# Load order of the first chunks, and the second pair's attention ahead of the feed-forward product

## The chip, the core and the metric

The kernel runs on one core of a Trainium2 chip. A core has five engines with instruction streams of their own, which meet at semaphores: TensorE (PE, matrix products; its weight loads are the row PEld), VectorE (DVE), ScalarE (ACT), GpSimd (POOL) and SyncE (SP). Each runs its own instructions in order. DMA engines move data between main memory (HBM) and the on-chip SBUF; products are collected in PSUM, in eight banks. The metric is the device time of one execution in microseconds (us).

## What is computed

Retention (linear attention with decay), written in the reference as a recurrence over 768 tokens, for 4 batches, 8 heads, head dimension 64; its result goes into a gated feed-forward layer.

```python
gamma = 1.0 - 2.0 ** (-5.0 - np.arange(H))
for t in range(S):
    state = gamma * state + einsum('bhd,bhe->bhde', k[:, :, t], v[:, :, t])
    y[:, :, t] = scale * einsum('bhd,bhde->bhe', q[:, :, t], state)
x = y.transpose(0, 2, 1, 3).reshape(3072, 512)
gate = 1 / (1 + exp(-(x @ w_gate)))     # 512 x 1536
out = (gate * (x @ w_val)) @ w_out      # 1536 x 512
```

## The kernel before

**Tiling.** Tokens are cut into 24 chunks of 128, six to a batch, and attention is done by chunk: scores of q and k within the chunk under a causal mask, times v (the *intra* product), plus q times the state of the chunks before (the *inter* product). The decay is folded into v, scaled by a table by token (tabr, tabv), and into y, multiplied by a table taby when it leaves PSUM. The feed-forward layer works on six tiles of 512 tokens, four chunks each: an *up* product by each of 12 column blocks of 128 (gate and value, wg and wv, four matmuls each; a sigmoid on ScalarE; a product on VectorE into hT), then eight half *down* products (6 matmuls each) from hT and wo. Operands are bf16, sums float32.

**The order is written by hand.** Every engine gets its instructions in the order in which the Python code issues them. After a prologue for tile 0, a loop goes over the tiles' groups (ups and downs), and `plan` names after which group of a tile a step of the attention of later chunks is put in: `step_t` (transposes of k and q, and scaling of v), `block` (scores, intra, state, inter) and `casts`.

**The prologue.** The first four chunks come in two pairs, a = 0 and a = 1 (chunks 0, 1 and 2, 3), loaded whole by `load_run` (L77): each partition holds two successive tokens of all heads. The names that matter:

- `kr`, `qr`, `vr`: the loads of a pair. Both `vr` share one buffer. `load_gate_val(s)` (L87) loads the slice s, 256 of 1536 columns, of wg and wv; `load_out` (L91) loads a quarter of wo; `load_chunk` (L62, L67, L68) loads k, q, v of a later chunk. All but the first `vr` are issued by GpSimd.
- `transpose_run` (L264, copy out L269 or L271), `scale_run` (L278; v times tabr), `scores_run` (L288), `masks_run` (L295), `inter_run` (L304), `intra_run` (L313), `state_run` (L325), `sum_run` (L332, L334), `state_out` (L208; the state cast to bf16 as zbd), `y_out_run` (L342; y times taby into xT, which the up product reads).
- `make_taby` (L144) makes taby by an exponential on ScalarE, `extend_taby` (L147) from another taby on GpSimd. ScalarE then changes its function table to sigmoid (L485).
- `up_columns` (L400) takes 256 tokens of two column blocks at once, `up` (L384) one block. `keep_on(n, warm)` (L429) issues n matmuls of the identity into a scratch bank; nobody reads them.

In the prologue before, the order of loads is vr0 (SyncE), kr0, qr0, kr1, wg and wv slice 0, vr1, qr1, slices 1 and 2, then slices 3 to 5, wo, chunks 4 to 7. Pair 0 is finished, up products of its 256 tokens begin (blocks 0 and 1), and among them pair 1 is scaled by VectorE, transposed, and brought through state, scores and intra; after blocks 2 to 5 of the first 256 tokens come blocks 0 to 5 of the second 256, and the loop begins at group 6.

Of the kernel before, what the change touches and what calls it, by code (L numbers as in the profile page):

```python
# [9 lines left out]
F32 = mybir.dt.float32  # L10
BF16 = mybir.dt.bfloat16
I32 = mybir.dt.int32
AX = mybir.ActivationFunctionType
# [4 lines left out]
def kernel(  # L18
# [10 lines left out]
    nc = tc.nc  # L29
# [45 lines left out]
    def load_run(x, a, dtype, eng, name):  # L75
        t = const.tile([128, H, 2 * D], dtype, name=name, tag=name, bufs=1)
        eng.dma_start(out=t, in_=x[0, :, a * 2 * C:(a + 1) * 2 * C, :].rearrange("h (p j) d -> p h (j d)", j=2))  # L77
        return t
# [5 lines left out]
    def load_gate_val(s):  # L84
        cols = slice(s * 256, (s + 1) * 256)
        for dst, w in ((wg, moe_w_gate), (wv, moe_w_val)):
            nc.gpsimd.dma_start(out=dst[:, :, cols],  # L87
                                in_=w.rearrange("(kk p) n -> p kk n", p=128)[:, :, cols])
# [18 lines left out]
    toky = const.tile([128, 384], I32, name="toky")  # L107
    nc.gpsimd.iota(toky, pattern=[[1, 384]], base=0, channel_multiplier=0)
    kr[1] = load_run(k, 1, BF16, nc.gpsimd, "kr1")
    load_gate_val(0)  # L110

    lgh = const.tile([128, H], F32, name="lgh")
    for h in range(H):
# [27 lines left out]
    def make_taby(c, pairs=range(NP)):  # L141
        n = taby[c].shape[2]
        for p in pairs:
            nc.scalar.activation(taby[c][:, p, :], toky[:, c * C:c * C + n], AX.Exp, scale=lgp[:, p:p + 1], bias=lsc)  # L144

    def extend_taby(c):
        nc.gpsimd.tensor_tensor(tab_y(c), tab_y(c - 3), gup.unsqueeze(2).to_broadcast([128, NP, C]), op=ALU.mult)  # L147
# [5 lines left out]
    def bank(shape, dt=F32):  # L153
        return pf.tile(shape, dt, tag="ff", name="ff")
# [121 lines left out]
    def scale_run(a, eng):  # L276
        vsr[a] = const.tile([128, H, 2, D], BF16, name=f"vsr{a}")
        eng.tensor_tensor(vsr[a], runs(vr[a]), tabr[:, a].unsqueeze(3).to_broadcast([128, H, 2, D]), op=ALU.mult)  # L278
# [17 lines left out]
                                    maskr2, op=ALU.mult)  # L296
        stA[a, n] = st

    def inter_run(g):
        a, c = divmod(g, 2)  # L300
        y[g] = bank([128, NP, C])
        if g > 0:
            for p in range(NP):
                nc.tensor.matmul(y[g][:, p, :], zbd[g - 1][:, p, :], qT[a][:, p, :, c * D:(c + 1) * D],  # L304
                                 start=(p == 0), stop=False, skip_group_check=True)

    def intra_run(a):
        for p in range(NP):
            for j in range(2):
                for c in range(2):  # L310
                    for i in range(2):
                        tok = slice(c * D, (c + 1) * D)
                        nc.tensor.matmul(y[2 * a + c][i * D:(i + 1) * D, p, :], vsr[a][tok, 2 * p + i, j, :],  # L313
                                         stA[a, p // 2][i][tok, p % 2, j, :],
                                         start=(a == 0 and c == 0 and p == 0 and j == 0), stop=True,
                                         skip_group_check=True)

    def state_run(a):
# [11 lines left out]
    def sum_run(g):  # L330
        if g == 0:
            nc.vector.tensor_copy(new_za(g), zz[g])  # L332
        else:
            nc.vector.tensor_tensor(new_za(g), za[g - 1], zz[g], op=ALU.add)  # L334

    def y_out_run(g, n=None):
        if 0 not in xT:
            xT[0] = new_xT()
        cols = slice(g % 2 * C, (g % 2 + 1) * C)
        of = slice(0, NP) if n is None else slice(2 * n, 2 * n + 2)  # L340
        in_runs = "x n (p j) -> x n j p"
        nc.vector.tensor_tensor(xT[0][:, g // 2, of, cols].rearrange(in_runs, j=2),  # L342
                                y[g][:, of].rearrange("x n (j p) -> x n j p", j=2),
                                tab_y(g)[:, of].rearrange(in_runs, j=2), op=ALU.mult)
# [29 lines left out]

    hT = {}

    def up(t, n1, lo=0, hi=512):
        if t not in hT:
            hT[t] = ffn.tile([128, NFF, 512], BF16, tag="hT", name="hT", bufs=2)
        ps = []  # L380
        for w in (wg, wv):
            u = bank([128, 512])
            for kk in range(KT):
                nc.tensor.matmul(u[:, lo:hi], w[:, kk, n1 * 128:(n1 + 1) * 128], x_cols(t, kk, lo, hi),  # L384
                                 start=(kk == 0), stop=(kk == KT - 1))
            ps.append(u)
        gs = ffn.tile([128, 512], F32, tag="gs", name="gs")
        nc.scalar.activation(gs[:, lo:hi], ps[0][:, lo:hi], AX.Sigmoid)  # L388
        nc.vector.tensor_tensor(hT[t][:, n1, lo:hi], gs[:, lo:hi], ps[1][:, lo:hi], op=ALU.mult)  # L389
# [37 lines left out]
    def keep_on(n, u):  # L427
        for _ in range(n):
            nc.tensor.matmul(u, ident, ident4, start=True, stop=True)  # L429
# [18 lines left out]

    make_taby(0)
    scale_run(0, nc.vector)  # L450
    maskr = const.tile([128, 2, 2, D], F32, name="maskr")
    nc.gpsimd.memset(maskr, 1.0)
    for i in range(2):
# [1 line left out]
        nc.gpsimd.affine_select(half, half, pattern=[[-1, 2], [1, 2], [2, D]], base=0, channel_multiplier=-2,  # L455
                                compare_op=ALU.is_ge, fill=0.0)
    maskr2 = maskr.rearrange("x j i p -> x (j i p)").unsqueeze(1).to_broadcast([128, 2, 4 * D])
    vr[1] = load_run(v, 1, F32, nc.gpsimd, "vr")
    qr[1] = load_run(q, 1, BF16, nc.gpsimd, "qr1")
    causal = const.tile([128, 128], F32, name="causal")  # L460
    nc.gpsimd.memset(causal, 1.0)
    nc.gpsimd.affine_select(causal, causal, pattern=[[1, 128]], base=0, channel_multiplier=-1,
                            compare_op=ALU.is_ge, fill=0.0)
    causal4 = causal.unsqueeze(1).to_broadcast([128, NP, 128])
    load_gate_val(1)
    load_gate_val(2)
    make_taby(2, range(2))
    warm = bank([128, 4, 128])
    keep_on(8, warm)
    kT[0], qT[0], kT[1], qT[1] = (new_run_T() for _ in range(4))  # L470
# [10 lines left out]
    masks_run(0, 0)  # L481
    masks_run(0, 1)
    transpose_run(kr[1], kT[1], [nc.scalar])
    make_taby(2, range(2, 4))
    nc.scalar.preload_act_table(AX.Sigmoid)  # L485
    inter_run(0)
    inter_run(1)
    keep_on(4, warm)
    intra_run(0)
    for n in range(2):  # L490
        for g in range(2):
            y_out_run(g, n)
    extend_taby(3)
    for s in range(3, NFF // 2):
        load_gate_val(s)
    extend_taby(4)
    extend_taby(5)
    for s in range(4):
        load_out(s)
    for g in range(4, 8):  # L500
        load_chunk(g)
    keep_on(2, warm)
    scale_run(1, nc.vector)
    up_columns(0, range(0, 2), 0, 256, 2)
    transpose_run(qr[1], qT[1], [nc.scalar, nc.vector])
    state_run(1)
    sum_run(2)
    state_out(2, za[2])
    scores_run(1)
    masks_run(1, 0)  # L510
    sum_run(3)
    masks_run(1, 1)
    inter_run(2)
    up_columns(0, range(2, 4), 0, 256)
    inter_run(3)
    intra_run(1)
    y_out_run(2)
    y_out_run(3)
    state_out(3, za[3])
    up_columns(0, range(4, 6), 0, 256)  # L520
    for n1 in range(0, 6, 2):
        up_columns(0, range(n1, n1 + 2), 256, 512)


# [3 lines left out]
    def downs(t):  # L528
        return [lambda sm=sm, i=i: down(t, sm, i) for sm in range(4) for i in range(2)]

    plan = {
        0: [(6, step_t, 4), (7, step_t, 5), (8, block, None, 4), (9, step_t, 6), (10, casts, 4), (10, step_t, 7),
            (12, block, 4, 6), (13, step_t, 8)],
        1: [(0, casts, 6), (1, step_t, 9), (3, block, 6, 8), (5, casts, 8), (7, scale_v, 10), (9, scale_v, 11),
            (11, block, 8, 10), (13, casts, 10), (14, scale_v, 12), (15, scale_v, 13), (18, block, 10, 12),
            (20, casts, 12)],
# [7 lines left out]
    for t in range(NT):  # L544
        groups = ups(t) + downs(t)
        if t == NT - 1:
            groups[-2:] = [lambda: last_down(t)]
        if t == 0:
            groups = groups[6:]
            for g in range(8, 12):  # L550
                load_chunk(g)
        if t == 1:
            groups[:6] = [lambda n1=n1: up(1, n1, 0, 256) for n1 in range(6)]
            groups[6:6] = [lambda n1=n1: up_columns(1, range(n1, n1 + 2), 256, 512) for n1 in range(0, 6, 2)]
            for g in range(12, 16):
                load_chunk(g)
        if t == 2:
            load_chunk(18)
            load_chunk(19)
        if t == 3:  # L560
            load_chunk(22)
            load_chunk(23)
        for i, group in enumerate(groups):
            if t == 1 and i == 0:
                for g in range(XBAR, 12):
                    xbar(g)
            if i == len(groups) - 9:
                for g in range(4 * t + 8, 4 * t + 12):
                    if 12 <= g < NG:
                        xbar(g)  # L570
            if t == 1 and i == len(groups) - 4:
                load_chunk(16)
                load_chunk(17)
            if t == 2 and i == len(groups) - 4:
                load_chunk(20)
                load_chunk(21)
            group()
            for at_group, step, *g in plan[t]:
                if at_group == i:
                    step(*g)  # L580
# [30 lines left out]
```

## Time and profile before

The median of five runs is 232.0 us (231.61 to 232.28).

| | |
|---|---|
| profiled execution | 232.0 us; its span, first to last instruction, 230.3 us |
| PE busy | 221.7 us (96%) |
| DVE, ACT, POOL busy | 119.1, 88.2, 75.3 us |
| up products (L384) by the chain that ended last | 47% of the span |
| down products (L418) by the same chain | 26% |
| up products by `up_columns` (L400) by the same chain | 5% |
| loads issued by GpSimd (queue q0) | 16.78 MB, 72.8% of 16 engines' span |

The page's second part cuts the span into 40 slices of 5.76 us; each digit is a busy share in tenths:

```profile
PE   4989999999999999999999999999999999999994
DVE  5579344449775937458336367637267620243301
ACT  5865333465553422526311532613532512434221
POOL 7998656999643444733230000000000000000000
DMA  7999999999999999999999642011100012100022
```

The busy time of a matmul row is modelled from its start; what counts for TensorE is the distance between starts. A wait is put in brackets behind a row of the timeline, with the instruction or the DMA that ended it.

### The profile page before, as it was taken

What the parts mean: (1) busy time and instruction counts of PE and PEld (TensorE: products, weight loads), DVE (VectorE), ACT (ScalarE), POOL (GpSimd) and SP (SyncE); (2) the same over time, 40 slices, a digit from 0 to 9 for tenths busy, and PEclk for the clock granted to TensorE, in tenths of its full rate; (3) what the DMA queues carried; (4) which work ended last, traced back from release to release, by engine and by line L of the source; (5) the groups of instructions that cost most, each with busy time, mean ns of one, the idle gap of its engine ahead of it and who ended that gap; (6) DMA issues with size and microseconds to landing.
All of it is one profiled execution on the core that took longest, in us unless ns stands there. A gap on an engine that the chain in (4) does not pass through costs nothing.

```text
span 230.3 us, 4518 instructions
## 1 busy us (share of the span) xinstructions
PE 221.7 (96%) x1822; PEld 121.2 (53%) x1834; DVE 119.1 (52%) x226; ACT 88.2 (38%) x161; POOL 75.3 (33%) x98
## 2 busy tenths in 40 slices
PE   4989999999999999999999999999999999999994
PEld 1557844558785455454445445445445454444444
DVE  5579344449775937458336367637267620243301
ACT  5865333465553422526311532613532512434221
POOL 7998656999643444733230000000000000000000
PEclk9999999999999999999999999999999999999999
DMA  7999999999999999999999642011100012100022
GB/s 137 182 229 196 199 205 212 226 245 243 186 123 125 150 135 157 262 136 116 117 101 248 156 88 48 0 50 65 73 3 0 0 48 91 46 0 3 0 91 93
DMA packets 75477, 27.56 MB, mean 120 GB/s; under 512 B 62016, under 2 KB 71104, under 8 KB 75456
## 3 DMA queue, kind: packets, MB, share of 16 engines
q0 software_dynamic: 55440, 16.78, 72.8%
q1 hardware_dynamic: 19872, 10.43, 26.1%
q8 instruction: 14, 0.23, 0.4%
q10 hardware_dynamic: 144, 0.07, 0.1%
q14 instruction: 7, 0.06, 0.1%
HBM read 28.31 MB, written 6.29 MB: 150 GB/s over the span
## 4 chain that ended last, share of the span: by engine, by line
PE 87%; POOL 5%; DMA 4%; ACT 1%; issue 1%; DVE 0%; POOLq 0%; ACTq 0%
PE ff L384 47%; PE ff L418 26%; PE ff L400 5%; DMA wv<-in_moe_w_val_dram 4%; PE ff L233 2%; PE ff L184 2%; PE ff L196 2%; PE ff L163 1%; PE ff L437 1%; POOL wg L87 1%; PE z L202 1%; POOL kr L77 1%; POOL qr L77 1%; POOL wv L87 1%; ACT gs L388 0%
## 5 line engine op out<-in xcount | busy, mean ns | idle before, releaser
L389 DVE TENSOR_TENSOR hT<-gs,ff 128x512 bf16<-128x512 f32 (+1 forms) x66 | 43.2, 663 | 58.9 <-PE ff L384 55.5
L384 PE MATMUL ff<-xT,wg 128*128 128x512 bf16 (+1 forms) x264 | 65.2, 369 | 0.0
L384 PE MATMUL ff<-xT,wv 128*128 128x512 bf16 (+1 forms) x264 | 65.2, 369 | 0.0
L388 ACT ACTIVATE gs<-ff 128x512 f32<-128x512 f32 (+1 forms) x66 | 38.0, 578 | 67.4 <-PE ff L384 61.4
L418 PE MATMUL ff<-wo,hT 128*128 128x512 bf16 x264 | 61.1, 379 | 1.0 <-issue 0.5
L418 PEld LDWEIGHTS <-hT 128*128 128x128 bf16 x276 | 26.4, 98 | 30.5
L384 PEld LDWEIGHTS <-wv 128*128 128x128 bf16 x264 | 25.9, 98 | 28.6
L384 PEld LDWEIGHTS <-wg 128*128 128x128 bf16 x264 | 25.4, 98 | 27.4
L423 ACT COPY ob<-ff 128x512 f32<-128x512 f32 x23 | 13.5, 585 | 49.6 <-PE ff L418 49.4
L251 DVE TENSOR_TENSOR xT<-ff,taby 128x512 bf16<-128x512 f32 x20 | 12.9, 687 | 24.7 <-PE ff L233 24.7
L62 POOL DMA_DIRECT2D vf<-in_v_dram x20 | 18.2, 908 | 21.2 <-DMA kn<-in_k_dram 12.5
L67 POOL DMA_DIRECT2D kn<-in_k_dram x20 | 17.8, 892 | 18.7 <-PE ff L384 13.4
L68 POOL DMA_DIRECT2D qn<-in_q_dram x20 | 17.9, 896 | 2.0 <-DMA wo<-in_moe_w_out_dram 1.6
L208 ACT CAST zbd<-za 64x256 bf16<-64x256 f32 x38 | 15.3, 403 | 7.0 <-DVE za L220 4.8
L175 DVE TENSOR_TENSOR vs<-vf,tabv 128x512 bf16<-128x512 f32 x20 | 13.4, 686 | 2.0 <-DMA vf<-in_v_dram 1.8
L189 DVE TENSOR_TENSOR stA<-ff,causal 128x512 bf16<-128x512 f32 x20 | 13.6, 682 | 0.0
L190 DVE TENSOR_TENSOR stB<-ff,causal 128x512 bf16<-128x512 f32 x20 | 13.6, 681 | 0.0
L400 PE MATMUL ff<-xT,wg 128*128 128x256 bf16 x72 | 9.5, 273 | 0.3 <-DVE xT L342 0.3
L400 PE MATMUL ff<-xT,wv 128*128 128x256 bf16 x72 | 9.5, 273 | 0.1
L429 PE MATMUL ff<-ident 128*128 128x512 bf16 x18 | 6.4, 492 | 3.0 <-POOL ident masks.py:199 3.0
L407 DVE TENSOR_TENSOR hT<-gs,ff 128x512 bf16<-128x512 f32 x9 | 6.1, 685 | 5.3 <-PE ff L400 4.0
L406 ACT ACTIVATE gs<-ff 128x512 f32<-128x512 f32 x9 | 5.2, 596 | 6.8 <-PE ff L400 6.7
(84 smaller groups left out, 155.4 us busy)
## 6 DMA issues: line engine op xcount, KB each, us to landing
out_dram<-ob SPq DMA_DIRECT2D x23, 256.0 KB, 2.2
vf<-in_v_dram POOLq DMA_DIRECT2D x20, 256.0 KB, 10.5
kn<-in_k_dram POOLq DMA_DIRECT2D x20, 128.0 KB, 12.4
qn<-in_q_dram POOLq DMA_DIRECT2D x20, 128.0 KB, 13.2
wg<-in_moe_w_gate_dram POOLq DMA_DIRECT2D x6, 256.0 KB, 8.5
wv<-in_moe_w_val_dram POOLq DMA_DIRECT2D x6, 256.0 KB, 9.5
wo<-in_moe_w_out_dram POOLq DMA_DIRECT2D x4, 384.0 KB, 11.5
vr<-in_v_dram SPq DMA_DIRECT2D x1, 512.0 KB, 4.2
```

Of the source, the lines that this page charges most:

```text
L62: nc.gpsimd.dma_start(out=vf[g], in_=src(v, g))
L67: nc.gpsimd.dma_start(out=kn[g], in_=src(k, g))
L68: nc.gpsimd.dma_start(out=qn[g], in_=src(q, g))
L189: nc.vector.tensor_tensor(stA[g], sc[g][0], causal4, op=ALU.mult)
L190: nc.vector.tensor_tensor(stB[g], sc[g][1], causal4, op=ALU.mult)
L208: nc.scalar.copy(zbd[g % 4][half, :, half], z[half])
L384: nc.tensor.matmul(u[:, lo:hi], w[:, kk, n1 * 128:(n1 + 1) * 128], x_cols(t, kk, lo, hi), start=(kk == 0), stop=(kk == KT - 1))
L388: nc.scalar.activation(gs[:, lo:hi], ps[0][:, lo:hi], AX.Sigmoid)
L389: nc.vector.tensor_tensor(hT[t][:, n1, lo:hi], gs[:, lo:hi], ps[1][:, lo:hi], op=ALU.mult)
L400: nc.tensor.matmul(u[:, i * n:(i + 1) * n], w[:, kk, n1 * 128:(n1 + 1) * 128], x_cols(t, kk, lo, hi), start=(kk == 0 and (rows == 1 or i = ...
L418: nc.tensor.matmul(o, hT[t][:, n1, sm * 128:(sm + 1) * 128], wo[:, n1, :], start=(n1 == 0), stop=(n1 == NFF - 1))
L423: nc.scalar.copy(ob, o)
```

## The change

- The loads of pair 1 (qr1 at once, vr1 after the first scaling) are issued before the weights; slice 0 of wg and wv comes after vr1 and the mask.
- v of pair 1 is scaled by GpSimd instead of VectorE, after the issue of weight slices 0 to 2.
- Transposes of q of pair 1, its scores and masks come before the first up product; the copy of the transposed q is done by ScalarE alone.
- taby of chunk 2 is made in one piece, after that copy; y of chunks 0 and 1 leaves PSUM in one instruction each instead of two.
- Up blocks 0 and 1 for the first 256 tokens are followed by inter, state and intra of pair 1. y of chunk 3 gets its intra product first; its inter product is put between the matmuls and the sigmoid of up block 2 (`between`), and ends the sum.
- Blocks 2 and 3 are done by `up` one at a time; of the first half-tile there are now four blocks instead of six in 256-token pieces. The loop begins at group 4 of tile 0, and the indices of the plan for tile 0 are two higher.
- The causal mask for later chunks is made after the issue of the weights. Of the `keep_on` matmuls six fall away and two come.

```diff
     kr[1] = load_run(k, 1, BF16, nc.gpsimd, "kr1")
-    load_gate_val(0)
+    qr[1] = load_run(q, 1, BF16, nc.gpsimd, "qr1")
...
-    def inter_run(g):
+    def inter_run(g, first=True):
         a, c = divmod(g, 2)
-        y[g] = bank([128, NP, C])
+        if first:
+            y[g] = bank([128, NP, C])
         if g > 0:
             for p in range(NP):
                 nc.tensor.matmul(y[g][:, p, :], zbd[g - 1][:, p, :], qT[a][:, p, :, c * D:(c + 1) * D],
-                                 start=(p == 0), stop=False, skip_group_check=True)
+                                 start=(first and p == 0), stop=not first, skip_group_check=True)
...
-                                         start=(a == 0 and c == 0 and p == 0 and j == 0), stop=True,
+                                         start=(2 * a + c in fresh and p == 0 and j == 0), stop=True,
...
-    def up(t, n1, lo=0, hi=512):
+    def up(t, n1, lo=0, hi=512, between=None):
...
+        if between:
+            between()
         gs = ffn.tile([128, 512], F32, tag="gs", name="gs")
...
     make_taby(0)
     scale_run(0, nc.vector)
+    vr[1] = load_run(v, 1, F32, nc.gpsimd, "vr")
...
-    vr[1] = load_run(v, 1, F32, nc.gpsimd, "vr")
-    qr[1] = load_run(q, 1, BF16, nc.gpsimd, "qr1")
-    causal = const.tile([128, 128], F32, name="causal")
...
+    load_gate_val(0)
     load_gate_val(1)
     load_gate_val(2)
-    make_taby(2, range(2))
+    scale_run(1, nc.gpsimd)
...
     transpose_run(kr[1], kT[1], [nc.scalar])
-    make_taby(2, range(2, 4))
-    nc.scalar.preload_act_table(AX.Sigmoid)
     inter_run(0)
     inter_run(1)
-    keep_on(4, warm)
-    intra_run(0)
-    for n in range(2):
-        for g in range(2):
-            y_out_run(g, n)
+    transpose_run(qr[1], qT[1], [nc.scalar])
+    intra_run(0, [0])
+    make_taby(2)
+    nc.scalar.preload_act_table(AX.Sigmoid)
+    y_out_run(0)
+    y_out_run(1)
+    scores_run(1)
+    masks_run(1, 0)
+    masks_run(1, 1)
+    keep_on(2, warm)
+    up_columns(0, range(0, 2), 0, 256)
+    inter_run(2)
+    state_run(1)
+    sum_run(2)
+    state_out(2, za[2])
+    sum_run(3)
     extend_taby(3)
     for s in range(3, NFF // 2):
         load_gate_val(s)
+    causal = const.tile([128, 128], F32, name="causal")
...
-    keep_on(2, warm)
-    scale_run(1, nc.vector)
-    up_columns(0, range(0, 2), 0, 256, 2)
-    transpose_run(qr[1], qT[1], [nc.scalar, nc.vector])
-    state_run(1)
-    sum_run(2)
-    state_out(2, za[2])
-    scores_run(1)
-    masks_run(1, 0)
-    sum_run(3)
-    masks_run(1, 1)
-    inter_run(2)
-    up_columns(0, range(2, 4), 0, 256)
-    inter_run(3)
-    intra_run(1)
+    y[3] = bank([128, NP, C])
+    intra_run(1, [3])
     y_out_run(2)
-    y_out_run(3)
+
+    def end_of_3():
+        inter_run(3, False)
+        y_out_run(3)
+
+    up(0, 2, 0, 256, end_of_3)
+    up(0, 3, 0, 256)
     state_out(3, za[3])
-    up_columns(0, range(4, 6), 0, 256)
-    for n1 in range(0, 6, 2):
+    for n1 in range(0, 4, 2):
         up_columns(0, range(n1, n1 + 2), 256, 512)
...
-            groups = groups[6:]
+            groups = groups[4:]
```

More of the change, by code (lines that the diff above doesn't have):

```diff
@@ L304, in inter_run, with intra_run @@
                 nc.tensor.matmul(y[g][:, p, :], zbd[g - 1][:, p, :], qT[a][:, p, :, c * D:(c + 1) * D],
-                                 start=(p == 0), stop=False, skip_group_check=True)
-    def intra_run(a):
+                                 start=(first and p == 0), stop=not first, skip_group_check=True)
+    def intra_run(a, fresh):
         for p in range(NP):
@@ L457 @@
     maskr2 = maskr.rearrange("x j i p -> x (j i p)").unsqueeze(1).to_broadcast([128, 2, 4 * D])
-    vr[1] = load_run(v, 1, F32, nc.gpsimd, "vr")
-    qr[1] = load_run(q, 1, BF16, nc.gpsimd, "qr1")
-    causal = const.tile([128, 128], F32, name="causal")
[L461 to L464, printed above, removed]
+    load_gate_val(0)
     load_gate_val(1)
     load_gate_val(2)
-    make_taby(2, range(2))
+    scale_run(1, nc.gpsimd)
     warm = bank([128, 4, 128])
@@ L495 @@
         load_gate_val(s)
+    causal = const.tile([128, 128], F32, name="causal")
+    nc.gpsimd.memset(causal, 1.0)
+    nc.gpsimd.affine_select(causal, causal, pattern=[[1, 128]], base=0, channel_multiplier=-1,
+                            compare_op=ALU.is_ge, fill=0.0)
+    causal4 = causal.unsqueeze(1).to_broadcast([128, NP, 128])
     extend_taby(4)
@@ L531 @@
     plan = {
-        0: [(6, step_t, 4), (7, step_t, 5), (8, block, None, 4), (9, step_t, 6), (10, casts, 4), (10, step_t, 7),
-            (12, block, 4, 6), (13, step_t, 8)],
+        0: [(8, step_t, 4), (9, step_t, 5), (10, block, None, 4), (11, step_t, 6), (12, casts, 4), (12, step_t, 7),
+            (14, block, 4, 6), (15, step_t, 8)],
         1: [(0, casts, 6), (1, step_t, 9), (3, block, 6, 8), (5, casts, 8), (7, scale_v, 10), (9, scale_v, 11),
```

## The prediction

> **What bounds the kernel now.** I read the page first (a busy TensorE, PE 96%), then the chain of waits, then the timeline of the first 45 us, where every changed line lies.
>
> The chain in order of time:
>
> ```profile
> 12.60 9.77 DMA wv<-in_moe_w_val_dram
> ...
> 22.42 6.29 PE ff L400 x56
> 28.70 10.36 PE ff L384 x48
> ```
>
> The chain comes from GpSimd's issues, runs through the third wv slice (on its way from 12.60 to 22.37), and from 22.42 on is TensorE alone, with only short waits to the end. So time is won only by bringing forward the point from which TensorE is dense. But the 9.77 us are not for the taking: TensorE waited 0.10 us for this slice and had worked nearly all the while. What it really lost there is small gaps, and filler: four and two L429 matmuls into a scratch bank (11.32 to 13.7), 0.21 us apiece.
>
> ```profile
> 14.02 0.60 PE L400 MATMUL ff<-xT,wg 128*128 128x256 bf16 x4 [0.30 <-DVE xT L342]
> 16.09 0.64 PE L264 MATMUL ff<-ident,qr 128*64 128x128 bf16 x16 [0.16 <-DMA qr<-in_q_dram]
> 17.41 0.88 PE L288 MATMUL ff<-qkT 64*64 64x128 bf16 x32 [0.32 <-ACT qkT L269]
> 38.90 1.46 PE L418 MATMUL ff<-wo,hT 128*128 128x512 bf16 x5
> 40.42 0.39 PE L163 MATMUL ff<-ident,qn 128*128 128x128 bf16 x4
> 42.16 0.39 PE L163 MATMUL ff<-ident,qn 128*128 128x128 bf16 x4
> ```
>
> The first number is the start, the second the length. To be seen: the gaps that the change aims at (0.30, 0.16, 0.32), the start of the first down product (38.90), and the transposes of q of chunks 4 and 5 (40.42, 42.16), which are not waiting.
>
> GpSimd and its loads:
>
> ```profile
> 13.36 1.08 POOL L147 TENSOR_TENSOR taby<-taby,gup 128x512 f32<-128x512 f32 x1
> ...
> 17.68 0.74 POOL L87 DMA_DIRECT2D wg<-in_moe_w_gate_dram  x1 [0.29 <-DMA wg<-in_moe_w_gate_dram]
> ...
> 31.98 0.87 POOL L68 DMA_DIRECT2D qn<-in_q_dram  x1 [0.54 <-DMA wo<-in_moe_w_out_dram]
> ```
>
> An issue waits for the load eight before it: the wg of 17.68 for the wg of 10.37, which took 7.0 us. Issue plus time to landing, load by load in the view of DMA issues, gives landings (us): kr0 6.5, qr0 8.0, kr1 10.5, wg0 11.8, wv0 13.2, vr1 14.8, qr1 16.0, wg1 17.4, wv1 18.7, wg2 20.1, wv2 22.4, wg3 23.1, then each 1.2 to 1.4 to wv5 29.8, the four wo 31.7 to 37.4, chunk 4 (k, q, v) 38.3, 39.2, 40.0, chunk 5 40.7, 41.6, 42.5. The page's DMA row is 9 from slice 2 to 23: one saturated line in order of issue.
>
> **The change, part by part.** *Load order.* The last q and v of the first four chunks take the places of the first weights; from the second weight slice on, order and number are the same. With the landing slots in the same places: qr1 about 12.0 (slots after kr1 are 1.2 to 2.4 long for loads of this kind, so 11.7 to 12.9), vr1 13.5, wg0 14.8, wv0 16.0, wg1 17.4 and so on. vr1 reuses the buffer that the scaling on VectorE reads until 6.33, so it goes out at 6.4, not 6.15.
>
> *v scaled by GpSimd.* No such row exists. The row nearest is L147, 1.08 us for 128x512 with two inputs: doubled, 2.1 us. From the other side, VectorE's own scaling row (1.23 us) as a floor. The Trainium skill (GPSIMD Engine Reference, Elementwise — side-by-side cycle accounting) speaks against the move: VectorE stays the rule, GpSimd takes 1.96 times as long, by it 2.4 us, and it gives 4.5 us for 2048 elements. I take 2.1. It starts when vr1 is there and its queue free (six weight issues of 0.76 from 8.7, so 13.3 to 13.6) and ends at 15.6; by the rule 16.0. Its reader, the state product, comes at 17.2, so both give the same total. Behind it on GpSimd stand L147 (to 16.7; its reader y_out(3) comes at 19.7), wg3 (issue 16.7 instead of 14.35), the other weights, the moved causal mask (0.5; read at 45 us) and wo (about 24 instead of 21.74). At 16.7 wg1 to wv2 are still to land, until 22.4: the line does not run dry, and from the chunk loads on the wait for the eighth load before sets the issue again. Cost nothing, while the scaling stays under about 5 us.
>
> *Attention of the second pair earlier.* TensorE: transposes of qr1 at 12.05 to 12.5 in place of four fillers; the intra product, whose last mask ends at 12.72 in both, done at 13.3. ScalarE copies the transposed q in one piece (1.02 us, as kT1's at 11.19): 12.7 to 13.7. Scores(1) 13.75 to 14.6, two fillers, then up for 0 to 256 of the first two columns: wg part 15.0 to 15.9, wv part from 16.05 (its landing) to 16.95. VectorE: y_out(0), (1) 13.3 to 14.65 (0.67 each), four masks to 17.15, hT to 17.95, two state sums (0.42) to 18.8, y_out(2) to 19.5. ScalarE: taby 1.8 us and the table load 1.28 end at 16.8, sigmoid 17.4, which hT awaits. TensorE meanwhile: inter(2) 17.2, state 17.55, intra(1) 18.1, up(2) with wv1 (18.7) to 19.2; ScalarE's cast of the summed state (0.82 after 18.4) releases inter(3) at 19.3; y_out(3) 19.75 to 20.45 beside up(3). So at 20.5 the second half of the tokens exists, and nothing is left but up products: four half-width pieces (8 matmuls, 0.875) and sixteen full ones (4 matmuls, 0.865): 20.5 + 3.5 + 13.84 = 37.84. The weights for it (wv2 at 24.9, wv5 at about 37) have landed long before. Against 38.90: **1.06 us won here**, in the first tile. Some 0.85 us of it are fillers (six go, two come, 0.21 each), the rest gaps.
>
> *What is late next.* After the first down part comes chunk 4, then chunk 5, whose loads come in the old order on the old line. Before, q of chunk 5 landed at 31.98 + 9.6 = 41.6 and was transposed at 42.16; a wait for a load ends about 0.05 after the landing (qr: 16.04, 16.09). So only 0.50 us can be passed on; k of chunk 5 allows 1.2, q of chunk 4 1.18, later chunks 1.5 or more (q of 7: landed 46.3, used 47.84). TensorE will stand about 0.55 us before the q of chunk 5. The rest of the program is the same work in the same order and TensorE-bound, with the plan's indices moved along by two.
>
> **Sum**: span 230.3 − 0.50 = 229.8. The profiled execution took 232.0 with 1.7 us around its span, and is itself the median of the runs; so **231.5**.
>
> **Rivals.** *Forecast*, the load of chunk 5 caps the gain: 231.5, own range 231.3 to 231.7. *The whole gain*: should the line move 0.6 us ahead (kr1 took 2.43 us where others of its kind took 1.5), nothing caps: 230.9. Against it: the line is full from 4 us on in both kernels, with equal bytes.
>
> *The chain to y_out(3) is late.* It runs qr1, ScalarE's copy, scores, masks, hT, sum, cast, inter(3), all in order on VectorE. If qr1 lands at 12.9 and the waits add up to 0.8, TensorE is dense from 21.3, and 0.2 is left: 231.8. Against it: masks have their slack until intra(1) at 17.5.
>
> *Slower, the line slips.* GpSimd issues nothing for about 3.3 us (13.4 to 16.7; before only 13.37 to 14.35), and then again 2.6 us from 21.2. If fewer loads in flight slow the line, or the scaling takes 6 us, all behind it lands later, q of chunk 5 too. The first 0.5 us cancels the gain; beyond it, each is lost whole. A slip of 0.9: 232.4. For it: before is only 0.5 us from the same bound. Against it: 5 us of loads queued at 16.7.
>
> *Slower, the clock.* The fillers kept TensorE busy. The granted clock is 9 tenths or more in all slices:
>
> ```profile
> PEclk9999999999999999999999999999999999999999
> ```
>
> The skill (TensorE: Matmul & The Clock Gate, What's actually happening) names a window of about 3.4 us of idling after which the clock halves. By the row, gaps to 0.3 us leave it; by the rule, the new ones (11.3 to 12.05, 13.3 to 13.75) are too short. If a window with a quarter idle should suffice, one window at half speed costs 1.7 us, and 1.7 − 1.06 makes 232.6; two windows, 234.3.
>
> **Chances.** Forecast 0.50, whole gain 0.12, late chain 0.12, slip 0.19, clock 0.07. About 0.2% (0.46 us) is what a measurement of this kernel tells from none; the line is 231.54. Of the forecast 0.37 lies below it, 0.13 above. Faster 0.49, same 0.25, slower 0.26. Range: from the whole gain to beyond the slip, 230.9 to 232.6, leaving out a second clock window and a longer slip.
>
> **What would show it.** Right: first L418-type product near 37.8; a wait on qn of chunk 5 of about 0.5 us just before 41.7; GpSimd's scaling near 2.1 us, ended before the state product; landings of chunk 5 within 0.3 us of 40.7, 41.6. Wrong: no wait there (then the chain of the first 20 us failed, if the down products start late), or a landing past 42.1 (the slip), or a clock row under 9 in slices 2 to 4.

## The result, and the profile after

The changed kernel takes 231.45 us (median of 43 runs, 230.93 to 233.7), the kernel before 232.02 (80 runs). The ratio is 0.9973, 95% interval 0.9962 to 0.9984: 0.6 us won, between 0.4 and 0.9. The profiled execution took 231.0, its span is 229.3; it lies near the quick end of the runs, while the profile of before was a median one, so what the two traces differ by (1.0 us) is more than the kernels do.

The chain of waits of the changed kernel (start, length, what), from GpSimd's scaling to the first down products:

```profile
13.61 1.90 POOL vsr L278
...
23.51 7.90 DMA wo<-in_moe_w_out_dram
31.71 9.61 DMA qn<-in_q_dram
41.76 1.29 PE ff L422 x6
```

Before, the chain left the loads at 22.4 and TensorE held it from there. Now it stays with loads until 41.3: the last link ahead of TensorE is q of chunk 5. GpSimd's pieces at its head are read here as order of issue, not as loss: slice 3 of wg went out 2.1 us later than before (16.45 against 14.35) and landed no later (22.9 against 23.1).

TensorE in the same trace (start, length, instruction, wait in brackets):

```profile
11.97 0.64 PE L264 MATMUL ff<-ident,qr 128*64 128x128 bf16 x16 [0.53 <-DMA qr<-in_q_dram]
13.72 0.64 PE L288 MATMUL ff<-qkT 64*64 64x128 bf16 x32 [0.55 <-ACT qkT L269]
...
16.18 1.05 PE L404 MATMUL ff<-xT,wv 128*128 128x256 bf16 x8 [0.40 <-DMA wv<-in_moe_w_val_dram]
...
37.89 1.46 PE L422 MATMUL ff<-wo,hT 128*128 128x512 bf16 x5
39.19 0.39 PE L163 MATMUL ff<-ident,kn 128*128 128x128 bf16 x4
39.41 0.39 PE L163 MATMUL ff<-ident,qn 128*128 128x128 bf16 x4
...
40.93 0.39 PE L163 MATMUL ff<-ident,kn 128*128 128x128 bf16 x4
41.36 0.40 PE L163 MATMUL ff<-ident,qn 128*128 128x128 bf16 x4
```

The three waits are new and longer than those of before, and yet the first down product starts at 37.89 instead of 38.90: the first two lie where there were fillers. By the distance between starts only two gaps of about 0.2 us are left behind them, ahead of the wv part of slice 1 (18.86) and ahead of the second half of the tokens (20.59). Transposes of k and q of one chunk start 0.22 us apart; in chunk 5 it is 0.43, so TensorE stood 0.21 us there, and 1.01 us of lead became 0.80 (42.16 to 41.36). It keeps this to the last product (223.55 against 224.34); the rest of the 1.0 us lies after it, in the last store and the closing. A bracket counts from the modelled end of the row before and so shows less than the distance between starts does: this wait of 0.21 us has none.

### The profile page after: what moved, and what is told of

Its sections match the earlier page's. It is cut to its first block, busy times and chain, and to the rows that moved or that the text cites. A ratio compares the mean times of both kernels' runs of the same rounds, so it can differ in the third digit from the quotient of the medians.

```text
span 229.3 us, 4480 instructions
## 1 busy us (share of the span) xinstructions
PE 220.2 (96%) x1802; PEld 118.8 (52%) x1814; DVE 117.6 (51%) x223; ACT 88.9 (39%) x162; POOL 77.2 (34%) x99
## 4 chain that ended last, share of the span: by engine, by line
PE 79%; DMA 12%; POOL 4%; ACT 1%; issue 1%; DVE 1%; POOLq 0%; DVEq 0%; ACTq 0%
PE ff L386 43%; PE ff L422 25%; DMA vr<-in_v_dram 5%; DMA qn<-in_q_dram 4%; DMA wo<-in_moe_w_out_dram 3%; PE ff L233 2%; PE ff L184 2%; PE ff L404 2%; PE ff L196 2%; POOL taby L147 1%; PE ff L441 1%; POOL wg L87 1%; POOL wv L87 1%; PE ff L163 1%; PE z L202 1%
## 5 line engine op out<-in xcount | busy, mean ns | idle before, releaser
L393 DVE TENSOR_TENSOR hT<-gs,ff 128x512 bf16<-128x512 f32 (+1 forms) x70 | 45.3, 656 | 61.0 <-PE ff L386 55.6
L386 PE MATMUL ff<-xT,wg 128*128 128x512 bf16 (+1 forms) x280 | 68.5, 367 | 0.0
L386 PE MATMUL ff<-xT,wv 128*128 128x512 bf16 (+1 forms) x280 | 68.5, 367 | 0.0
L392 ACT ACTIVATE gs<-ff 128x512 f32<-128x512 f32 (+1 forms) x70 | 40.0, 573 | 70.2 <-PE ff L386 64.2
L386 PEld LDWEIGHTS <-wv 128*128 128x128 bf16 x280 | 27.3, 98 | 29.9 <-DMA wv<-in_moe_w_val_dram 0.3
L386 PEld LDWEIGHTS <-wg 128*128 128x128 bf16 x280 | 26.8, 98 | 28.6
L427 ACT COPY ob<-ff 128x512 f32<-128x512 f32 x23 | 13.5, 585 | 49.7 <-PE ff L422 49.4
L175 DVE TENSOR_TENSOR vs<-vf,tabv 128x512 bf16<-128x512 f32 x20 | 13.4, 685 | 2.8 <-DMA vf<-in_v_dram 2.8
L165 ACT ACTIVATE qkT<-ff 128x1024 bf16<-128x1024 bf16 x6 | 6.1, 1024 | 2.1 <-PE ff L163 2.0
L404 PE MATMUL ff<-xT,wv 128*128 128x256 bf16 x48 | 6.2, 273 | 0.4 <-DMA wv<-in_moe_w_val_dram 0.4
L233 PE MATMUL ff<-stA,vs 128*64 128x128 bf16 x80 | 6.3, 222 | 0.0
L233 PE MATMUL ff<-stB,vs 128*64 128x128 bf16 x80 | 6.3, 222 | 0.0
```

The costliest lines, as they stand in the source:

```text
L233: nc.tensor.matmul(y[g][i * D:(i + 1) * D, p, :], vs[g][:, 2 * p + i, :], st[:, p, :], start=(first and p == 0), stop=True, skip_group_che ...
L427: nc.scalar.copy(ob, o)
```

## The experiments

Two theories from the prediction stand behind all of them: the *early chain* (TensorE is ready about 1.0 us sooner by the rearranged first 20 us) and the *cap* (q of chunk 5 lets 0.5 of it pass).

### Is the load of chunk 5 the cap? Asking for it later

```diff
-        0: [(8, step_t, 4), (9, step_t, 5), (10, block, None, 4), (11, step_t, 6), (12, casts, 4), (12, step_t, 7),
+        0: [(8, step_t, 4), (10, step_t, 5), (11, block, None, 4), (12, step_t, 6), (13, casts, 4), (13, step_t, 7),
             (14, block, 4, 6), (15, step_t, 8)],
```

> The changed kernel with the transposes of chunk 5 and the score block of chunks 4 and 5 one half down product later (plan indices 10 and 11 for tile 0 instead of 9 and 10; the transposes of 6 and 7 and the casts move by one too, the next block stays). The loads are as they were; only TensorE asks 1.3 us later for q of chunk 5. Theory (this load caps the gain): no wait of TensorE between 38 and 48 us, the 1.0 us at the first down product comes through to the end, ratio to before about 0.9957, 231.0. Rival (the cap is the load line as such, and moves to the next load that is waited for, as with k and q loaded first): a wait of 0.3 us or more at q of chunk 6 or 7, ratio 0.997 or more.

Measured: 231.06 us, ratio 0.9952 (0.9931 to 0.9973). TensorE in its trace:

```profile
37.72 1.46 PE L422 MATMUL ff<-wo,hT 128*128 128x512 bf16 x5
...
39.46 2.75 PE L422 MATMUL ff<-wo,hT 128*128 128x512 bf16 x12
42.05 0.39 PE L163 MATMUL ff<-ident,kn 128*128 128x128 bf16 x4
42.27 0.39 PE L163 MATMUL ff<-ident,qn 128*128 128x128 bf16 x4
```

Two half down products run through, then k and q of chunk 5 are 0.22 us apart, and so are those of chunks 6 and 7: no load is waited for. The loads came no sooner than otherwise (q of chunk 5 issued at 31.54, landed 9.7 us on). But the move has a price of its own, which the expectation left out. Only one half down product, not two, now stands between the transposes of chunk 7 and the next scores, and TensorE (here its weight load) waits for ScalarE's copy of them:

```profile
50.46 0.23 PEld L184 LDWEIGHTS <-qkT 64*128 64x128 bf16 x8 [0.22 <-ACT qkT L165]
```

So in these two traces the move wins nothing: from the first down product to the last group of products it is 185.66 us in both (37.72 to 223.38; for the change 37.89 to 223.55), and 185.44 in the kernel before (38.90 to 224.34). It can win only where the wait for the load is longer than 0.22 us. The expected ratio was 0.9957; the measured one agrees, but the medians beside it (231.06 and 231.76) give 0.9970. This version is quicker than the kernel before. That it is quicker than the change is not shown: the two intervals touch.

> The kernel before with the same step moved. Theory: there TensorE came 0.5 us after the load, so nothing is won: ratio 1.000 within 0.0015. Rival (in ordinary executions the load binds before as well): ratio 0.998 or less.

Measured on the kernel before, with the same step moved: 232.05 us, ratio 1.0003 (0.9985 to 1.0021). Nothing is won where TensorE is late, and its trace has the same price: 185.66 us (39.32 to 224.98). The pair is the best evidence on the cap. With the step in its old place the two kernels are 0.57 us apart by their medians; with it moved in both they are 0.99 us apart (231.06 and 232.05, run beside each other), about the whole lead. The direction is the one expected, but the size is not clear of noise: the two ratios, put together, give 0.995 with an interval of about 0.003 to each side (an estimate from the two intervals), and the ratio of the change, 0.9973, lies within it.

### The same cap, attacked from the other side: loading it sooner

```diff
-    for g in range(4, 8):
+    load_kq(4)
+    load_kq(5)
+    load_v(4)
+    load_v(5)
+    for g in range(6, 8):
         load_chunk(g)
```

> The changed kernel with the loads of chunks 4 and 5 in the order k4, q4, k5, q5, v4, v5 (was k4, q4, v4, k5, q5, v5). Theory (the load of q of chunk 5 caps the gain: in the profile TensorE was 1.01 us ahead at the first down product, 37.89 against 38.90, and 0.78 ahead after the transposes of chunk 5): q5 lands one slot (about 0.9 us) earlier, near 40.4, the wait before its transposes goes, scores of chunk 4 start near 42.8 instead of 42.99, and the whole 1.0 us comes through: about 231.2. Rival (nothing waits for this load in earnest, the gain is what the first 20 us give and is spent): 231.45, scores at 42.99. Second rival (the v loads, now 0.9 to 1.4 us later, bind the state product): a wait of TensorE before the state product at 43.5, 231.5 or more.

Measured: 231.72 us, ratio 0.9988 (0.9972 to 1.0003): no better than the change, perhaps worse. In its trace, a quick execution of 231.28, the step worked where it was aimed, and TensorE waited later:

```profile
40.69 0.39 PE L163 MATMUL ff<-ident,kn 128*128 128x128 bf16 x4
40.91 0.39 PE L163 MATMUL ff<-ident,qn 128*128 128x128 bf16 x4
...
42.52 0.62 PE L184 MATMUL ff<-qkT 64*128 64x128 bf16 x16
...
46.37 0.39 PE L163 MATMUL ff<-ident,kn 128*128 128x128 bf16 x4
47.38 0.40 PE L163 MATMUL ff<-ident,qn 128*128 128x128 bf16 x4 [0.62 <-DMA qn<-in_q_dram]
```

Chunk 5 no longer waits and the scores start at 42.52 instead of 42.99 (0.24 us of this is an earlier first down product, 37.65), but now q of chunk 7 is missing. It landed at 47.3, after 46.0 in the trace of the change. Whether the new order did that is open: in the run without six fillers (below), whose loads have the order of the change, it landed at 47.1. Neither theory named this wait; the second rival looked for one at the state product, where there is none. On the kernel before:

> The kernel before with the same order of the loads of chunks 4 and 5. Theory: before had 0.5 us of slack at this load, so nothing: 232.0, first down product at 38.9, scores at 43.77. Rival (the loads bind before as well): 231.7 or less.

Measured: 232.18 us, ratio 1.0010 (0.9992 to 1.0028), first down product 38.99, scores 43.86: nothing won, as expected.

### And made worse: one more load ahead of chunk 4

```diff
+    extra = const.tile([128, H, D], BF16, name="extra")
+    nc.gpsimd.dma_start(out=extra, in_=src(k, 4))
     for g in range(4, 8):
         load_chunk(g)
```

> The changed kernel with one more load of 128 KB (k of chunk 4 into a tile that nobody reads) issued just before the loads of chunk 4, so that all behind it land about 0.85 us later. Theory (the load line is the bound at chunk 5): the slip is paid in full, about 232.3, with a wait of about 1.1 us before the transposes of q of chunk 5. Rival (TensorE's own chain of the first 20 us sets the end): the first down product stays at 37.9 and the time at 231.5 to 231.7.

Measured: 232.09 us, ratio 1.0014 (0.9998 to 1.0029). Against the ratio of the change, 0.9973, that is 0.0041 or 0.95 us lost for one slot of 0.85 (each ratio is to the kernel before, run beside it). In its trace the first down product is even sooner (37.34) and nothing comes of it:

```profile
38.97 0.40 PE L163 MATMUL ff<-ident,kn 128*128 128x128 bf16 x4 [0.17 <-DMA kn<-in_k_dram]
39.86 0.40 PE L163 MATMUL ff<-ident,qn 128*128 128x128 bf16 x4 [0.49 <-DMA qn<-in_q_dram]
...
42.26 0.40 PE L163 MATMUL ff<-ident,qn 128*128 128x128 bf16 x4 [0.48 <-DMA qn<-in_q_dram]
```

TensorE follows the landings one by one and passes the q of chunk 5 at 42.26, 0.90 us later than the change did. The wait is split over three places; the expectation had it in one.

> The kernel before with the same extra load. Theory: 0.85 us of slip less 0.55 us of slack: 232.3, the same time as the changed kernel with the extra load, so that the gain of the change is gone altogether. Rival: the difference of 0.57 us between the two kernels stays: 232.0 for this one, 231.5 for the other.

Measured: 232.56 us, ratio 1.0032 (1.0017 to 1.0046). The kernel before loses 0.0032, or 0.74 us, where 0.3 was expected; so the gain shrinks (0.0018 lies between the two, 0.4 us, with overlapping intervals) but is not gone. Since both kernels lose about as much, this pair does not settle the cap. Nor does the trace explain the 0.74 us: it is of one of the slowest executions (234.24), and what it lost, it lost earlier. vr of the second pair landed at 15.9 instead of 14.8, with the same issue time and far ahead of the extra load, and q behind it at 17.2; TensorE stood 1.85 us for it and then ran 3.4 us at half its clock. So late, it came to q of chunk 5 at 44.57, 1.4 us after its landing at 43.2. Only two of the 22 executions had such a clock. Why the others lost more than 0.3 us is open.

### The early chain: who scales v, and where the last inter product stands

```diff
-    scale_run(1, nc.gpsimd)
...
     masks_run(1, 1)
+    scale_run(1, nc.vector)
```

> The changed kernel with v of the second pair scaled by VectorE, after the four masks of the second pair, instead of by GpSimd. Theory (VectorE's chain masks, hT, sums, y_out(3) sets when TensorE becomes dense; GpSimd's 1.90 us were hidden): this chain gets 1.23 us longer, less the 0.4 us that hT waited for the sigmoid: y_out(3) ends near 21.4 instead of 20.54, the first down product is near 38.8, and about 0.7 us of the time is lost: 232.1. GpSimd's first issue after slice 2 comes at 14.5 instead of 16.45, and the loads of chunk 5 land as before. Rival (which engine scales makes no difference): 231.45. Second rival (GpSimd's long instruction delays the loads, so that taking it away wins): 231.1, with loads of chunk 5 0.3 us or more earlier.

Measured: 232.12 us, ratio 1.000 (0.9979 to 1.0021): the whole gain is gone. VectorE and TensorE in its trace:

```profile
16.87 1.20 DVE L278 TENSOR_TENSOR vsr<-vr,tabr 128x1024 bf16<-128x1024 f32 x1
18.00 0.67 DVE L411 TENSOR_TENSOR hT<-gs,ff 128x512 bf16<-128x512 f32 x1
```

```profile
18.12 0.22 PE L327 MATMUL z<-vsr,kr 64*64 64x64 bf16 x2 [0.72 <-DVE vsr L278]
```

hT, which had to wait for the scaling, starts at 18.00 instead of 17.33, and TensorE's state product stands 0.72 us for the scaled v. The last y leaves at 21.2 instead of 20.5, and the first down product starts at 38.55. The loads of chunk 5 land within 0.4 us of where they did (q at 41.7). So an engine that takes 1.90 us for what another does in 1.20 was the right one here: VectorE's chain has no room there, GpSimd's queue has.

```diff
-    y[3] = bank([128, NP, C])
-    intra_run(1, [3])
+    inter_run(3)
+    intra_run(1, [])
     y_out_run(2)
-    def end_of_3():
-        inter_run(3, False)
-        y_out_run(3)
-    up(0, 2, 0, 256, end_of_3)
+    y_out_run(3)
+    up(0, 2, 0, 256)
```

> The changed kernel with the last inter product ahead of the intra product and of the up products, as before the change, instead of between the matmuls of up block 2. Theory (TensorE would stand for the state of chunk 2 to be summed and cast, which ends at 19.2): TensorE waits about 1.4 us from 17.8 on, its dense stretch starts about 0.8 us later, first down product near 38.7, and past the cap of the load 0.55 us are lost: 232.0. Rival (the place of the inter product does not matter, the wait is elsewhere anyway): 231.45, first down product at 37.9.

Measured: 232.60 us, ratio 1.0027 (1.0008 to 1.0045). The wait is as expected:

```profile
19.00 0.40 PE L305 MATMUL ff<-qkT,zbd 128*128 128x128 bf16 x4 [1.43 <-ACT zbd L208]
```

The first down product is at 38.97, 1.08 us after the change's, and the last products come 0.86 us after its own: the later start, less the wait for q of chunk 5, which falls away. Without this one piece the change would be a loss. The time is 0.6 us above the expectation, and this trace does not explain that: it is of an execution of 232.05, the quickest of its twenty. What the others lose beyond it is open.

### The fillers and the clock

```diff
     sum_run(1)
-    keep_on(2, warm)
...
     state_out(1, za[1])
-    keep_on(2, warm)
...
     masks_run(1, 1)
-    keep_on(2, warm)
```

> The changed kernel without the last six of its filler matmuls (three times two); the first eight stay. Theory: the fillers lie in waits, for the loads of q0 and of the first weights and for copies; 231.45 within 0.2, granted clock 1.00 in the first 30 us. Rival (the fillers keep the clock up): a clock under 1 in the first 25 us and 0.6 us or more lost: 232 and over. Second rival (fillers cost their 0.21 us each): first down product up to 0.6 us earlier.

Measured: 231.36 us, ratio 0.9971 (0.9956 to 0.9987): no different from the change. Its trace is the best view of the cap, since TensorE begins the down products as in the changed kernel (37.92) and the load came at another time:

```profile
40.96 0.39 PE L163 MATMUL ff<-ident,kn 128*128 128x128 bf16 x4
41.79 0.40 PE L163 MATMUL ff<-ident,qn 128*128 128x128 bf16 x4 [0.45 <-DMA qn<-in_q_dram]
```

q of chunk 5 was issued at 32.20 and took 9.5 us, so it landed at 41.7 instead of 41.3. By the distance between starts TensorE stood 0.61 us (0.83 less 0.22), and it is 0.43 us later here than in the trace of the change. This execution took 231.39, about the median.

```diff
     inter_run(1)
-    keep_on(4, warm)
     intra_run(0)
...
-    keep_on(2, warm)
     scale_run(1, nc.vector)
```

> The kernel before without the four fillers ahead of the first intra product and the two ahead of the first up product, the six that the change removes. Theory (they lay in waits: the last mask ends at 12.72, and y_out at 14.0): 232.0 within 0.2, first down product at 38.8 to 38.9. Rival (the change gains by dropping 0.85 us of fillers): 231.4 or less, first down product near 38.1.

Measured on the kernel before: 232.95 us, ratio 1.0025 (1.0006 to 1.0045). It became slower. The stretches of its trace, then of the kernel before (each row: from and to, length, busy time and count of PE, PEld, DVE, ACT, POOL, granted clock, DMA share, GB/s):

```profile
11.20:14.65 3.45, 2.05 (x47) 1.48 (x42) 2.98 (x7) 3.26 (x5) 3.45 (x5) 1.00 1.41 260
14.65:18.05 3.40, 3.40 (x29) 2.38 (x27) 2.00 (x3) 0.60 (x1) 3.00 (x5) 0.50 1.48 195
```

```profile
11.20:14.65 3.45, 3.12 (x48) 1.75 (x47) 2.96 (x7) 3.17 (x4) 3.45 (x5) 1.00 1.41 259
14.65:18.05 3.40, 2.89 (x89) 2.17 (x90) 2.57 (x4) 1.19 (x2) 3.10 (x5) 1.00 1.49 195
```

Without the fillers TensorE is busy for 2.05 of 3.45 us, and then runs at half its clock for 3.4 us. One such window lowers an execution's mean clock to 0.993 (0.5 × 3.4 of 230), which can be counted: in this kernel 8 of 12 executions, in the runs of the kernel before beside it 1 of 63, in the changed kernel 4 of 44, and in the changed kernel without six fillers 2 of 20. With the dip an execution of the changed kernel takes 232.3 in the median, without it 231.4. The fillers of before were not dead weight: they had held the clock, and the rearrangement does most of that with real work. Nor did they cost time: the four executions without a dip have a median of 232.2, those of the kernel before 231.95.

```diff
+    keep_on(2, warm)
     transpose_run(qr[1], qT[1], [nc.scalar])
     intra_run(0, [0])
+    keep_on(2, warm)
```

> As the run with the step moved, and with two filler matmuls ahead of the transposes of q of the second pair and two ahead of its scores, where TensorE stood for 0.53 and 0.55 us. Theory: they fit into these waits (0.43 us each), first down product within 0.1 us; the executions with a granted clock of 0.993 (four of 44 with the changed kernel) go, the median stays: ratio 0.9955. Rival (fillers delay what follows them): first down product 0.2 us or more later, ratio 0.9965 or more.

Measured: 231.27 us, ratio 0.9976 (0.9959 to 0.9992). None of 22 executions had the dip. That says little: the three runs that alter the changed kernel only further on (k and q first, the extra load, the step moved) had none in 45 either, without these fillers. The median is no better than without them. The trace doesn't decide between the two: TensorE was already 1.0 us late at the first scores (10.52 instead of 9.48), ahead of the edit. Inconclusive.

### The order of the loads

```diff
     kr[1] = load_run(k, 1, BF16, nc.gpsimd, "kr1")
-    qr[1] = load_run(q, 1, BF16, nc.gpsimd, "qr1")
+    load_gate_val(0)
...
     vr[1] = load_run(v, 1, F32, nc.gpsimd, "vr")
+    qr[1] = load_run(q, 1, BF16, nc.gpsimd, "qr1")
...
-    load_gate_val(0)
     load_gate_val(1)
```

> The changed kernel with the loads in their old order: weight slice 0 after the second k, then v and q of the second pair. Theory (the changed order of work needs the changed order of loads): q lands near 16.0, the transposes, and behind them on TensorE the first intra product, wait about 4 us from 11.4 on, the first down product comes near 41.7, and a window of idling may halve the clock for 3.4 us on top: ratio 1.012 to 1.02, 234.7 to 236.5. Rival (the order of work alone gives the gain): ratio 0.9973.

Measured: 236.83 us (four runs), ratio 1.0186 (1.0149 to 1.0222).

```profile
16.41 1.06 PE L264 MATMUL ff<-ident,qr 128*64 128x128 bf16 x16 [4.92 <-DMA qr<-in_q_dram]
```

TensorE stood for 4.92 us, from 11.5 to 16.4. The clock was at half from 12.5 on, a microsecond into the wait, until 22.7, and the first down product came at 44.1. The expectation named both losses and had put the second at one window of 3.4 us; in the trace it was three (mean clock 0.976), in the other three executions, by their mean clock of 0.985 or 0.986, two.

## Why the prediction was right

**The bound.** Dense from the first up products on, so that only the start can be won: right. The first down product was forecast at 37.84 and came at 37.89. Two readings beside it were off, without weight in the sum: for the third wv slice TensorE lost 0.28 us, not 0.10 (the products start 1.15 us apart, 21.27 and 22.42, where 0.87 is usual), and the DMA row is 9 in slices 2 to 22.

**What was won there.** The prediction put 0.85 of its 1.06 us down to fillers that fall away. As a count of TensorE's work this holds, as a cause it does not: without the same six fillers the kernel before was no quicker. They stood in waits, and real work now stands in their place.

**The load order.** Landings forecast for qr1, vr1, wg0, wv0: 12.0, 13.5, 14.8, 16.0; measured 11.9, 13.4, 14.6, 16.1. That the same bytes ahead of a point of the line give the same landing there held within 0.2 us.

**v on GpSimd.** 2.1 us was taken from the row of L147; it took 1.90. The ratio of the Trainium skill (GPSIMD Engine Reference, Elementwise — side-by-side cycle accounting) would have given 2.4 (an estimate, 1.96 times VectorE's 1.23); here it is 1.90 to 1.20 us, 1.6 times. By either it ends before its reader comes, as the prediction said (it ended at 15.5, the reader came at 17.4), and with VectorE doing it the gain was gone. GpSimd issued nothing from 13.36 to 16.45, and the line did not run dry: slice 3 of wg landed at 22.9, before at 23.1.

**The chain to y_out(3).** Forecast end 20.45, measured 20.54.

**The cap.** Right in place: TensorE waits for q of chunk 5 in the trace of the change and in that without six fillers, and not in the kernel before. In size the time agrees: 0.50 us forecast, 0.57 by the medians. That it agrees so closely has luck in it, since the 0.50 was read from one trace. In the trace that came with the change it was smaller than forecast (0.21 us of wait, not 0.55), since that execution's q of chunk 5 landed at 41.3. In the other traces with the loads in the change's order it landed between 41.2 and 41.7 (five of them), in those of before's order at 41.4, 41.6 and 41.9: the scatter from one execution to the next is as large as what is at stake, and neither order is seen to be the sooner one.

**The rivals.** The slipping line was kept off by the loads that were queued. The clock was held to be unlikely by a rule that only a window of idling halves it; it does happen in four of 44 executions of the changed kernel, at about 0.9 us each (the prediction had put one window at 1.7), and in two of three of the kernel before without fillers. So the rule was too mild and the price too high; at four of 44 the median does not feel it. Where in the changed kernel it happens no trace shows.

What stays open: why the kernel before loses 0.74 us, not 0.3, to one more load, why the version with the inter product outside is 0.6 us slower than expected, and what the new order of loads alone would do for the kernel before, which was not run.

## What to carry to other kernels

A lead won early is worth what the next shared resource lets through: read, for each later consumer of a full load line, how long after the landing it came, and take the smallest distance as the limit of the gain. When a load is the cap, its consumer can ask later or the load can come sooner; follow either to the next place that gets tight. Here the first took the wait away and brought one of 0.22 us at the next scores, the second had a new wait two chunks on, and neither was shown to beat the change. An elementwise operation belongs on the engine whose queue has room at that time, even if, as here, it takes 1.6 times as long there.

## What the hardware showed that was not expected

The clock halved although TensorE had not been idle for a whole window. In three traces a stretch at a clock of 0.50 or 0.51 followed one in which TensorE was busy for 2.05 of 3.45 us (the kernel before without fillers, longest gap 0.83 us), 1.86 of 3.40 (the kernel before with one more load) and 1.80 of 3.50 (the old loads). But so small a share did not always halve it. From the changed kernel without six fillers (columns as above):

```profile
13.00:16.40 3.40, 1.86 (x44) 1.32 (x42) 3.38 (x6) 3.35 (x7) 3.33 (x4) 1.00 1.42 190
```

The clock stayed at 1.00 in the 3.4 us behind this too. The Trainium skill (TensorE: Matmul & The Clock Gate, What's actually happening) has the clock fall after at least one idle window of about 3.4 us, and calls the window free-running, not started by the kernel. The length agrees (3.4 us at half clock, or 10.2, three times as much), and a window that runs on its own would let some executions of one kernel dip and others not, as the counts show. That the window has to be idle does not agree with the three traces. Where the threshold lies no run shows.
